# An attention and feed-forward kernel: the last whole group's sums and stores are listed ahead of the last products, and the steps behind unit 18 stand in a new order

## The chip, the cores and the metric

The kernel runs on one core of one Trainium2 chip. The metric is the device time of one execution in microseconds (us). Before the change it is 647.43 us, the median of three runs (647.06 to 649.99).

The engines are named as in the profile: PE is TensorE's matmul, PEld its weight load, DVE is VectorE, ACT is ScalarE, POOL is GpSimd, and SP is SyncE, whose queue issues most DMAs. Each engine works through its own list of instructions in order, and waits at an instruction until what it needs from the others is there.

## The reference

The first half is an attention over 32 memory slots for each of 8 batches and 8 heads (576 rows, 64 columns); the second is a feed-forward layer with a leaky ReLU on all 4608 rows:

```python
def _attn_ref(q, k, v, phi):
    a = np.exp(phi - np.max(phi, axis=2, keepdims=True))
    a = a / (np.sum(a, axis=2, keepdims=True) + 1e-09)
    k_m = np.einsum('bhsm,bhsd->bhmd', a, k)
    v_m = np.einsum('bhsm,bhsd->bhmd', a, v)
    scores = 1.0 / np.sqrt(q.shape[-1]) * np.matmul(q, k_m.transpose(0, 1, 3, 2))
    attn = softmax(scores)            # with 1e-09 in the denominator
    return np.matmul(attn, v_m)

x = attn_out.transpose(0, 2, 1, 3).reshape(4608, 512)
h = x @ w_in                          # w_in 512 x 2048
out = np.maximum(0.01 * h, h) @ w_out # w_out 2048 x 512
```

All arrays are float32.

## The kernel before

The program is one long list of named **steps**, written out in two tables of text, `OPENING` and `LATER`. At the end the kernel calls the steps in the order of the tables (`run(OPENING.split())`, `run(LATER.split())`) under a manual schedule: a step's instructions are put at the end of the lists of the engines that it uses. So the tables alone set the order of work on each engine. Two steps that use different engines don't delay each other by their order in the table; only the order within an engine, and the waits for data and buffers, count.

A step's name is a kind, a number and a part:

- `a2.C10`, `a6.E1` and so on are the attention of one batch. `phi`, `kv0` to `kv3`, `q0`, `q1` are its loads on SP. `A1` (line 595) and `A2` (610, 614) take the maxima of phi on DVE, `B...` the exponentials, `C10` (701) the products with k and v on PE, `D...` small transposes and scales (`D4`: 352 to 817; `D5`, `D6`: 823 and 828, the two halves of the operand vT), `E1`, `E3` (864) the scores on PE, `E20` to `E23` (909) their flips on DVE, and `S01` to `S08` (931 and on) the softmax.
- `W20` and the like fold w_in with the memory values of a batch (2) for a quarter of the hidden columns (0): `p` products on PE (1023), `h` high parts on ACT (1056), `l` low parts on DVE (1062). With it the up product runs on the attention weights.
- `i...` and `o...` prepare w_in and w_out: loads, rounding, splits into float16 high and low parts (419, 424, 444 to 450).
- Units 0 to 23 are the up and down products of the first two batches, in three groups of 384 rows: `P` up products on PE (1136), `V` leaky ReLU on ACT (1143), `C` and `L` high and low parts on DVE (1153, 1157), `O` down products on PE (1218). `Z` stores a group.
- Units 0 to 55 in small letters are the same for the other six batches, in 14 groups (G = 3 to 16) of 256 rows with 4 units each: `p` up products on PE (1263), `v` leaky ReLU on ACT (1279), `s` sums of its blocks on DVE (1300), `c` high parts on ACT (1304), `l` low parts on DVE (1308), `d` down products on PE (1331). A whole group takes seven block products instead of eight, so the results are sums of the seven: `x15.p` (ACT, 1341) and `x15.0` to `x15.3` (DVE, 1344, 1346, 1349, 1351) for group 15. `z15.0`, `z15.1` scale its two tiles of 128 rows (ACT, 1355) and store them: four DMAs of 64 KB each on SP (1185).
- Group 16 has 128 rows only (units 52 to 55). Its down products (line 1368) make two halves of 256 columns. `end0` scales the first half on ACT (1202), `end1` the second on DVE (1204); each half goes out in four DMAs of 32 KB, two from SP's queue and two from ACT's.

Up and down products in float16 run three times: high by high, high by low, low by high. So a `d` step of groups 3 to 15 is 6 matmuls of 128x256. The up products of groups 3 to 16 write two halves of one PSUM bank in turn, so `p52.2` must wait until `v52.0` has read what `p52.0` wrote. The operands of the down products lie in three buffers (`k % 3`), so unit 54's are written over unit 51's. The three PSUM banks of the down products are handed from one group to the next when the sums have read them.

Of the kernel before, what the change touches and what calls it, by code (L numbers as in the profile page):

```python
# [71 lines left out]
W01.l0 C9 o2.k0 a1.S12 o3.n3 P11.0 L9 V10.1 O8.1 a2.A3 o2.s1 o2.l0 o2.s2 P11.1 W01.h1 o2.k2 C10  # L72
# [14 lines left out]
a2.S05 i3.k2 a3.B10 i3.k0 a2.S06 O20.1 V22.0 a3.B20 W20.l0 W22.p W22.h0 W22.l0 a3.B3 O21.0 a3.C10
i3.l1 i3.l0 a2.S07 a3.C2 C22 a3.C30 a2.S08 p0.0 p0.1 O21.1 v0.0 p0.2 v0.2 L22 o1.n3 a3.C3k O22.0
a3.C31 v0.1 a4.phi i3.l2 a3.q0 V23.1 p0.3 C23 W23.p a3.C4 W23.h1 p1.0 v1.0 O22.1 v0.3 c0.0 p1.1 p1.2
W22.h1 L23 a4.A1 W23.h0 W23.l1 v1.2 s0 W23.l0 v1.1 a3.q1 c0.1 O23.0 p1.3 l0.0 W22.l1 a3.D2 v1.3  # L90
a3.D4 a3.D11 a3.D5 O23.1 p2.0 a3.D10 d0.0 l0.1 a3.Q1 p2.1 a3.Q0 Z2.0 d0.5 Z2.2 c1.0 a3.D6 v2.1 d0.3
v2.0 d0.4 l1.0 a3.D3 Z2.1 p2.2 a3.E1 a3.E22 a3.E3 s1 d0.1 a4.A2 v2.2 a3.E21 p2.3 p3.0 a3.E20 d1.0
# [5 lines left out]
a4.B3 p6.1 W31.h0 v6.1 x3.1 d4.1 a4.C10 a3.S07 p6.2 p6.3 a4.q1 s5 v6.2 d4.2 x3.2 v6.3 d3.6 l5.0
a4.C2 x3.3 d4.5 c5.1 p7.0 p7.1 a4.C30 a4.C31 d4.6 l5.1 v7.0 a4.q0 d5.0 p7.2 c6.0 d5.1 a3.S08 s6 v7.1
d5.5 d4.3 l6.0 v7.2 a4.C3k p7.3 p8.0 c6.1 d6.0 a4.D10 d4.4 a5.phi W31.l0 v7.3 d5.3 c7.0 l6.1 s7 p8.1  # L100
v8.1 d5.6 d6.5 d5.2 v8.0 a4.Q1 z3.1 l7.0 p8.2 z3.0 d6.1 a4.Q0 d5.4 a4.C4 a4.D3 d6.2 p8.3 a5.A1 v8.3
v8.2 c8.0 a4.E1 a4.E20 d7.0 c7.1 a4.E21 a4.E22 a5.A2 p9.0 v9.0 a5.A4 d6.3 a4.E3 l7.1 W32.p p9.1
W32.h0 s8 W32.h1 p9.2 v9.1 a4.E23 c8.1 d6.4 W32.l1 d7.1 a5.kv3 p9.3 a5.kv0 W32.l0 l8.0 v9.2 d6.6
# [6 lines left out]
d11.1 z4.0 s12 p13.1 d11.5 p13.2 v13.2 d11.0 d11.6 a5.B3 v13.1 W40.l0 W41.l1 c12.1 d10.3 p13.3 l12.1  # L110
v13.3 c12.0 a5.C10 d11.2 s13 l12.0 p14.0 p14.1 c13.0 v14.1 x5.p a5.q1 W41.l0 a4.S06 a5.C2 v14.0
d10.4 x5.0 c13.1 l13.0 d11.3 d11.4 d12.0 d12.1 p14.2 x5.1 x5.2 p14.3 a5.C30 d12.3 d12.2 x5.3 a4.S07
v14.2 v14.3 p15.0 p15.1 c14.0 v15.0 d12.4 v15.1 a5.C31 a5.C3k d12.5 a5.C4 p15.2 l14.0 a6.phi a5.D2
p15.3 a5.q0 d13.0 v15.2 v15.3 a5.Q1 l13.1 d12.6 s14 c15.0 a4.S08 z5.1 p16.0 d14.0 p16.1 v16.1 d13.1
# [18 lines left out]
p27.0 d23.6 d23.4 l25.0 v27.0 x8.0 a7.phi x8.1 v26.3 p27.1 x8.2 x8.3 c25.1 v27.1 a6.C4 d25.0 d24.5
p27.2 c26.0 p27.3 d24.3 d24.4 l25.1 a6.q1 v27.2 p28.0 s26 a6.C3k d24.6 d24.1 v27.3 a6.D10 l26.0
v28.0 c27.0 d24.2 c26.1 d25.1 d25.2 d25.3 d26.1 a6.Q0 p28.1 a6.Q1 a6.D3 p28.2 a6.E1 l26.1 v28.1
d25.4 a6.E20 d25.5 s27 p28.3 a6.D2 d26.3 z8.1 d25.6 d26.5 d26.6 v28.2 l27.0 p29.0 a6.D4 d26.4 c27.1
l27.1 a6.D11 a6.E21 v28.3 d26.2 v29.0 p29.1 z8.0 a6.D5 a7.A1 p29.2 c28.0 d26.0 v29.1 d27.0 d27.3
a6.D6 l28.0 a6.E22 d27.1 os5 s28 p29.3 W60.p a7.A2 a6.E3 v29.3 x9.p a6.E23 d27.2 x9.0 x9.1 a7.kv1
# [1387 lines left out]
```

## Time and profile before

| | us |
|---|---|
| median of three runs | 647.43 |
| the profiled execution's own time | 646.6 |
| its span (first to last instruction on the core) | 644.5 |
| PE busy | 626.9 (97%) |
| DVE busy | 526.7 (82%) |
| ACT busy | 383.7 (60%) |
| POOL busy | 33.8 (5%) |

The granted clock of TensorE was 0.997 of full speed over the span. The profile's groups give a line, engine, operation, tiles and count, then busy time and the mean of one, then the idle time of the engine ahead of them. A timeline row gives start, length, engine, line, operation and count; what stands in brackets is the engine's idle time ahead of it and who ended it. Ends of matmuls are modelled. `SPq` and `ACTq` are the issues of DMAs in these engines' queues.

### The profile page before, as it was taken

Reading aid. Unit: us, or ns where it says so; the run is one execution under the profiler, and the core shown is the slowest. Engines: PE = TensorE matmul, PEld = TensorE weight load, DVE = VectorE, ACT = ScalarE, POOL = GpSimd, SP = SyncE. Lnnn points to the kernel's source line nnn. Section 1 sums busy time; section 2 is a strip of 40 time slices with the busy share of each in tenths; the row PEclk is TensorE's granted clock in tenths of the full one; section 3 lists DMA queues with packets and bytes.
Section 4 is the critical chain, followed back from the end, with each engine's and each line's share of the span. In section 5 each row is a group of like instructions: output and inputs, shape, how many; then the busy total and the mean of one; then the engine's idle time right before and its main releaser. Section 6 shows DMA issues by size and latency. Waiting matters only on the chain.

```text
span 644.5 us, 17207 instructions
## 1 busy us (share of the span) xinstructions
PE 626.9 (97%) x7324; PEld 478.4 (74%) x7324; DVE 526.7 (82%) x870; ACT 383.7 (60%) x670; POOL 33.8 (5%) x38
## 2 busy tenths in 40 slices
PE   6799999999999999999999999999999999999996
...
GB/s 261 404 390 301 242 46 46 116 75 38 160 46 90 73 155 38 109 157 19 100 118 18 42 13 97 74 56 138 53 18 35 84 26 3 17 18 34 17 19 49
DMA packets 85500, 61.16 MB, mean 95 GB/s; under 512 B 62000, under 2 KB 68656, under 8 KB 85424
## 3 DMA queue, kind: packets, MB, share of 16 engines
...
q8 instruction: 57, 0.93, 0.6%
...
## 4 chain that ended last, share of the span: by engine, by line
PE 81%; DVE 10%; DMA 6%; ACT 2%; issue 1%; SPq 0%; DVEq 0%; ACTq 0%
PE po L1331 30%; PE ph L1263 21%; PE po L1218 11%; PE ph L1331 5%; PE ph L1136 4%; DMA arena<-in_moe_w_in_dram 4%; PE pa L1023 3%; PE pa L701 2%; PE po L1368 2%; PE pa L864 1%; DMA arena<-in_v_dram 1%; DVE arena L1300 1%; DVE arena L1157 1%; DVE arena L444 1%; DVE wo L424 1%
## 5 line engine op out<-in xcount | busy, mean ns | idle before, releaser
L1331 PEld LDWEIGHTS <-arena 128*128 128x128 f16 x2184 | 210.6, 98 | 29.2 <-issue 5.1
L1279 ACT ACTIVATE wi<-ph,g_sc 128x256 f32<-128x256 f32 (+1 forms) x224 | 96.1, 465 | 163.0 <-PE ph L1263 157.6
L1263 PE MATMUL ph<-a,w_mem 128*128 128x256 f16 (+3 forms) x1440 | 142.3, 246 | 0.5 <-ACT wi L1279 0.5
L1263 PEld LDWEIGHTS <-w_mem 128*128 128x128 f16 x1440 | 114.0, 98 | 15.4 <-issue 5.2
L1331 PE MATMUL po<-wo,arena 128*128 128x256 f16 x936 | 121.0, 273 | 0.4 <-DVE obs L1349 0.3
L1331 PE MATMUL po<-arena 128*128 128x256 f16 x936 | 120.0, 273 | 0.0
L1218 PE MATMUL po<-wo,arena 128*128 128x512 f16 (+1 forms) x396 | 107.6, 419 | 0.3 <-DVE arena L1157 0.3
L1308 DVE TENSOR_TENSOR arena<-arena 128x1024 f16<-128x1024 f32 x52 | 65.1, 1251 | 9.1 <-ACT arena L1304 9.1
L1308 DVE TENSOR_TENSOR arena<-wi,arena 128x768 f16<-128x768 f32 (+1 forms) x60 | 52.2, 878 | 22.4 <-ACT arena L1304 22.3
L1304 ACT CAST arena<-arena 128x1024 f16<-128x1024 f32 x52 | 54.3, 1045 | 9.0 <-DVE arena L1300 9.0
L1218 PEld LDWEIGHTS <-arena 128*128 128x128 f16 x324 | 31.1, 98 | 36.6 <-issue 2.5
L1300 DVE TENSOR_TENSOR arena<-wi 128x256 f32<-128x256 f32 x104 | 43.5, 459 | 5.0 <-ACT wi L1279 3.2
L1304 ACT CAST arena<-wi 128x768 f16<-128x768 f32 (+1 forms) x60 | 46.0, 774 | 2.2 <-PE po L1331 1.6
L1136 PE MATMUL ph<-a,w_mem 128*128 128x192 f16 (+2 forms) x288 | 46.9, 307 | 0.2 <-DVE w_mem L1062 0.2
L1300 DVE TENSOR_TENSOR arena<-wi,arena 128x256 f32<-128x256 f32 x104 | 43.8, 421 | 1.8
L988 POOL TENSOR_TENSOR a<-t,a 128x1024 f16<-128x1024 f32 (+2 forms) x16 | 23.8, 1506 | 407.8 <-ACT a L983 407.8
L1331 PE MATMUL ph<-wo,arena 128*128 128x256 f16 x312 | 42.1, 273 | 0.0
L1143 ACT ACTIVATE arena<-ph,g_sc 128x384 f32<-128x384 f32 x36 | 20.3, 577 | 20.3 <-PE ph L1136 18.9
L1136 PEld LDWEIGHTS <-w_mem 128*128 128x128 f16 x264 | 23.3, 98 | 10.8 <-issue 1.2
L1062 DVE SCALAR_TENSOR_TENSOR w_mem<-pa,w_mem 128x512 f16<-128x512 f32 x40 | 26.8, 683 | 4.8 <-ACT w_mem L1056 4.8
L1023 PE MATMUL pa<-wi,vT 64*32 64x512 f16 (+1 forms) x704 | 29.0, 420 | 1.0 <-ACT vT L808 1.0
L1056 ACT ACTIVATE w_mem<-pa 128x512 f16<-128x512 f32 x40 | 23.2, 597 | 5.9 <-PE pa L1023 5.9
...
## 6 DMA issues: line engine op xcount, KB each, us to landing
...
```

The source lines that it names most:

```text
L988: nc.gpsimd.tensor_tensor(piece(lo, tb), piece(t2, tb), piece(hi, tb), ALU.subtract)
L1023: nc.tensor.matmul(pf[g][cols, :], lhs, rhs, start=(n == 0), stop=(n == len(passes) - 1), tile_position=(g * D, hh * M),)
L1056: nc.scalar.activation(tiles(halves(w16(b, j), g)[:, 0]), w(g), AF.Copy, scale=ws)
L1062: nc.vector.scalar_tensor_tensor(tiles(t[:, 1]), w(g), ws, tiles(t[:, 0]), ALU.mult, ALU.subtract)
L1136: nc.tensor.matmul(ph[:, t0:t0 + n * SB], lhs, rhs, start=(m == 0), stop=(m == len(seq) - 1))
L1218: nc.tensor.matmul(pos["32" if full(G, u) else G][t], lhs, rhs, start=(f == 2 * u0 and m == 0), stop=(f == 2 * u1 - 1 and m == len(seq) - 1),)
L1263: nc.tensor.matmul(ph[:, t0:t0 + n], lhs, rhs, start=(m == 0), stop=(m == len(seq) - 1))
L1279: nc.scalar.activation(dst, ph, AF.Prelu, scale=g_sc2[:, j:j + 1], alpha=SLOPE)
L1300: nc.vector.tensor_tensor(gt[:, x], y, z, op)
L1304: nc.scalar.copy(dst[:, 0], src)
L1308: nc.vector.tensor_tensor(dst[:, 1], src, dst[:, 0], ALU.subtract)
L1331: nc.tensor.matmul(acc, g[:, x, s, u], rhs, start=(h == 0 and j == 0 and u == 0 and m == 0), stop=(j == NQ - 1 and u == 1 and m == 2), ski ...
```

## The change

Only the two tables of text are changed; every function stays as it is, and every step is called once, as before. `OPENING` has three moves in its middle: `i3.ld1` and `i2.h2` ahead of `u1.O1`, `o2.h2` and `a1.kv1` against their neighbours, `u3.V1` behind `a1.E1`. `LATER` has two moves ahead of unit 18 (`a2.A3`, `o0.k0`) and a new order from there to its last row. The steps `x15.3`, `z15.0` and `z15.1` stand behind `l55.1`, between `d54.2` and `d54.3`, before the change; they stand behind `p55.2` and from there to `d53.2` after it.

```diff
 OPENING = """
...
-o2.t0 i1.b f02.1 o2.h2 u2.P1 o2.y1 u3.V0 f02.2 u2.O0 a1.A1 a1.A2 u4.P0 a1.kv1 i3.h1 a1.A3 a1.B0
+o2.t0 i1.b f02.1 u2.P1 a1.kv1 o2.y1 u3.V0 f02.2 u2.O0 o2.h2 a1.A1 a1.A2 u4.P0 i3.h1 a1.A3 a1.B0
...
-a1.C31 u4.V1 u3.V1 a1.D3 i3.y0 u5.P0 a1.E1 a2.phi i3.h0 i3.t0 a1.C4 i3.h2 a1.E22 u3.O1 i3.y2 o3.ld2
+a1.C31 u4.V1 a1.D3 i3.y0 u5.P0 a1.E1 a2.phi u3.V1 i3.h0 i3.t0 a1.C4 i3.h2 a1.E22 u3.O1 i3.y2 o3.ld2
...
 LATER = """
...
-o0.n3 o0.n2 os1 i1.k2 P18.0 a2.E23 i1.l0 a2.E20 V18.0 C19 Z1.2 C18 L19 P21.0 P21.1 Z1.1 L18 Z1.0
-i1.k1 V21.1 i2.k0 a2.D11 O16.0 O16.1 O17.0 a2.E21 a2.S01 o0.m0 i0.l2 i1.l2 i1.l1 V21.0 P23.0 a2.D2
-i2.k1 a2.D4 a2.D5 O17.1 a3.kv2 P20.0 a3.kv0 C21 V20.0 L21 O18.0 V23.0 a2.D6 P20.1 V20.1 a3.A1 a3.A2
...
+o0.n3 o0.n2 os1 i1.k2 a3.kv2 a3.A1 a2.E21 P18.0 V18.0 C19 Z1.0 C18 a2.E20 Z1.1 Z1.2 P21.1 i1.l0
+P21.0 i1.k1 a3.kv0 O16.0 O16.1 L19 a2.E23 V21.0 V21.1 a2.D2 O17.0 i0.l2 O17.1 P23.0 i2.k0 a2.D11
+a2.D4 a2.S01 a3.A2 L18 i1.l2 i1.l1 a3.kv1 a2.D5 P20.0 a2.D6 O18.0 a3.A4 C21 W20.p V20.0 i2.k1 P20.1
...
-v51.1 p51.2 p51.3 z14.1 v51.3 l50.0 v51.2 l49.1 d49.5 s50 d49.1 c50.1 d48.4 c51.0 p52.0 p52.1 l51.0
-v52.0 d49.2 v52.1 d49.3 d49.4 c52.0 z14.0 p52.2 p52.3 l50.1 s51 d50.1 v52.2 d50.0 v52.3 p53.0 p53.1
-d50.3 c51.1 v53.0 d50.4 d50.2 v53.1 d49.6 p53.2 d51.1 l51.1 l52.0 v53.2 c52.1 d51.3 d50.5 d51.2
-p53.3 p54.0 d51.0 v53.3 d50.6 p54.1 x15.p d51.4 c53.0 x15.0 d51.5 v54.1 v54.0 x15.1 p54.2 l53.0
-p54.3 l52.1 v54.3 v54.2 d51.6 x15.2 c54.1 c53.1 d52.0 p55.0 d52.1 d52.2 d52.3 c54.0 d53.0 v55.0
-l54.0 p55.1 l53.1 p55.2 l54.1 d53.1 v55.2 v55.1 c55.0 l55.0 d53.2 d53.3 d54.0 d54.1 p55.3 v55.3
-d54.2 c55.1 l55.1 x15.3 z15.0 z15.1 d54.3 d55.0 d55.1 end0 d55.2 d55.3 end1
+l50.0 d48.4 d49.3 p51.2 p51.3 v51.3 d48.1 d48.2 d48.6 d49.4 v51.2 p52.0 p52.1 s50 c50.1 c51.0 l50.1
+s51 z14.0 d49.1 v52.0 v52.1 c51.1 d49.0 p52.2 p52.3 v52.2 v52.3 d49.2 d50.1 d50.2 p53.0 d50.3 d50.4
+l51.1 z14.1 c52.0 d50.0 p53.1 v53.1 v53.0 d51.3 l51.0 d51.0 d49.5 x15.p p53.2 p53.3 d51.1 l52.0
+v53.2 v53.3 d51.2 p54.0 p54.1 x15.0 d51.4 v54.1 c53.0 x15.1 v54.0 x15.2 d49.6 d50.5 p54.2 p54.3
+c52.1 l53.0 d52.0 d52.1 c54.0 l52.1 v54.2 v54.3 p55.0 p55.1 v55.0 d52.2 d52.3 v55.1 d50.6 d51.5
+d51.6 c53.1 l53.1 c54.1 p55.2 x15.3 p55.3 v55.2 d53.0 d53.1 l54.1 l54.0 v55.3 c55.0 l55.0 z15.0
+d53.2 z15.1 c55.1 l55.1 d53.3 d54.0 d54.1 d54.2 d54.3 d55.0 d55.1 end0 d55.2 d55.3 end1
 """
```

More of the change, by code (lines that the diff above doesn't have):

```diff
@@ L71 @@
 o2.m0 P10.0 V9.1 L8 W01.h0 P10.1 i0.k0 Z0.1 W11.p Z0.0 o3.s3 o3.m3 o2.n0 Z0.2 o2.k1 V10.0 O8.0
[L72 removed]
+W01.l0 C9 o2.k0 a1.S12 o3.n3 a2.A3 P11.0 L9 V10.1 O8.1 o2.s1 o2.l0 o2.s2 P11.1 W01.h1 o2.k2 C10
 W01.l1 a1.S13 O9.0 a2.B10 V11.0 o2.m1 o2.m2 o2.n1 W11.h1 V11.1 L10 O9.1 o2.s3 a2.kv0 W11.h0 W11.l1
@@ L77 @@
 P14.0 C13 o1.s1 o1.n0 L13 V14.0 O11.1 o1.m1 o1.s2 P14.1 V14.1 a1.S18 C14 O12.0 o1.n1 o1.s3 L14 a2.B3
-P15.0 o1.l2 o1.m2 O12.1 V15.0 o0.k0 P16.1 V16.1 P15.1 o1.n2 P16.0 a2.C2 a3.phi o0.l0 a2.C30 V15.1
+P15.0 o1.l2 o1.m2 O12.1 V15.0 P16.1 o0.k0 V16.1 P15.1 o1.n2 P16.0 a2.C2 a3.phi o0.l0 a2.C30 V15.1
 C15 o0.s3 P17.1 V16.0 C16 o0.s0 L16 o0.k1 a2.C3k o0.l1 o0.s1 O13.0 o0.k2 L15 a2.Q1 o0.l2 O13.1 O14.0
@@ L87 @@
[L87 to L92, printed above, removed]
@@ L98 @@
[L98 to L103, printed above, removed]
@@ L110 @@
[L110 to L114, printed above, removed]
@@ L133 @@
[L133 to L138, printed above, removed]
@@ new lines @@
+P21.0 i1.k1 a3.kv0 O16.0 O16.1 L19 a2.E23 V21.0 V21.1 a2.D2 O17.0 i0.l2 O17.1 P23.0 i2.k0 a2.D11
+a2.D4 a2.S01 a3.A2 L18 i1.l2 i1.l1 a3.kv1 a2.D5 P20.0 a2.D6 O18.0 a3.A4 C21 W20.p V20.0 i2.k1 P20.1
+a2.S02 W20.h1 O18.1 W20.l1 L21 V20.1 i2.l1 i2.k2 a2.S03 o1.m3 i2.l0 W20.h0 a3.A3 W21.p C20 i2.l2 L20
+P22.0 O19.0 O19.1 i3.k2 W20.l0 W21.h1 O20.0 V22.0 a2.S04 W21.l1 W21.h0 a3.B10 o0.m0 P22.1 W22.p
+a2.S05 i3.k0 W21.l0 a2.S06 i3.k1 V23.0 O20.1 O21.0 i3.l1 V22.1 P23.1 W22.h0 W22.l0 a3.B20 a3.B3
+a3.C10 a3.C2 a2.S07 a2.S08 p0.0 V23.1 o1.n3 p0.1 C23 O21.1 W22.h1 i3.l0 v0.0 v0.1 p0.2 C22 a3.C30
@@ new lines @@
+a3.C3k L22 i3.l2 p0.3 v0.3 v0.2 o0.n0 O22.0 a3.C31 a3.C4 c0.0 l0.0 p1.0 p1.1 a4.phi v1.0 O22.1 a3.q0
+a3.D2 v1.1 L23 a3.D10 s0 p1.2 a3.D4 W22.l1 a3.D11 p1.3 a3.D5 a3.D6 v1.3 O23.0 a3.q1 v1.2 p2.0 a3.Q0
+a4.A1 W23.p v2.0 c0.1 a3.Q1 O23.1 l0.1 p2.1 p2.2 d0.0 W23.h1 W23.l1 W23.h0 W23.l0 Z2.2 d0.5 v2.1 s1
+Z2.0 a3.D3 a4.A2 p2.3 d0.1 d0.6 v2.3 a3.E1 a3.E22 v2.2 Z2.1 c1.1 c1.0 a3.E3 p3.0 p3.1 d0.2 a3.E23
+a3.E20 d0.3 l1.0 W30.p v3.1 v3.0 d1.1 p3.2 l1.1 p3.3 a3.E21 s2 c2.0 d1.0 v3.3 a3.S01 l2.0 W30.h1
@@ new lines @@
+W30.l1 v3.2 c3.0 c2.1 l3.0 a4.A4 l2.1 d0.4 d1.3 a4.A3 p4.0 p4.1 d2.0 v4.1 W31.p v4.0 s3 d1.2 p4.2
+d1.5 a4.kv0 v4.2 d1.6 d2.5 W31.h1 c3.1 a4.kv1 d3.0 a3.S02 W31.h0 W30.h0 p4.3 l3.1 p5.0 v4.3 v5.0
+d1.4 d2.3 d2.1 a4.kv3 a4.B10 p5.1 x3.p p5.2 d2.6 a3.S03 os2 c4.0 s4 v5.2 c4.1 W31.l1 v5.1 d2.2 d3.1
+d3.2 d2.4 l4.0 p5.3 W31.l0 l4.1 d3.5 p6.0 a4.kv2 a4.B20 d3.3 a4.C10 a3.S04 a3.S05 v5.3 c5.0 x3.0
+v6.0 p6.1 d3.4 v6.1 d3.6 p6.2 p6.3 l5.0 a4.B3 a4.C2 a3.S06 W30.l0 x3.1 s5 x3.2 d4.0 d4.1 d4.2 v6.3
+a3.S07 v6.2 x3.3 d5.1 c5.1 p7.0 p7.1 c6.0 l5.1 v7.1 a4.q0 a4.C30 a5.phi a3.S08 d4.5 d4.3 d4.6 d5.0
@@ new lines @@
+v7.0 p7.2 p7.3 a4.C3k d4.4 a4.D10 d5.5 l6.0 d5.6 v7.3 v7.2 p8.0 p8.1 a4.C31 s6 c7.0 a4.q1 v8.0 d5.3
+a4.Q0 d5.2 c6.1 p8.2 a5.A1 d6.0 v8.1 a4.D3 l7.0 d5.4 p8.3 v8.2 v8.3 c8.0 a4.Q1 l6.1 s7 d6.1 a4.E1
+d6.3 z3.0 z3.1 a4.E22 a4.E20 p9.0 p9.1 d6.5 a4.E3 a4.E21 a4.C4 c7.1 W32.p v9.0 W32.h1 l7.1 d7.0
+a4.E23 p9.2 W32.h0 a5.A2 W32.l0 d6.2 a5.kv3 v9.1 W32.l1 v9.2 d6.4 a4.D2 p9.3 v9.3 a4.D4 W33.p W33.h0
+d7.1 s8 d6.6 a4.D11 p10.0 l8.0 d7.2 x4.p d7.3 c8.1 a4.D5 c9.0 d7.5 W33.l0 p10.1 d7.4 d8.0 v10.0
+v10.1 l8.1 p10.2 a4.D6 x4.0 p10.3 l9.0 W33.h1 W33.l1 os3 W40.p a5.A4 v10.2 d8.5 p11.0 W40.h1 s9
@@ new lines @@
+p14.1 p14.2 a5.q1 x5.p x5.0 x5.1 v14.1 d12.0 d12.3 v14.2 p14.3 x5.2 l13.0 d12.1 d12.2 a5.C30 p15.0
+d12.4 s13 c13.1 a5.C3k d13.1 x5.3 v15.0 d12.5 d13.0 v14.3 p15.1 p15.2 d12.6 l13.1 d13.5 s14 W41.l0
+a5.Q0 a5.C31 a6.kv0 d13.6 a5.C4 c14.0 l14.0 a4.S08 v15.2 v15.1 p15.3 v15.3 c15.0 a5.Q1 d13.2 d13.3
+p16.0 z5.1 a5.D2 a5.D4 v16.0 a5.D10 a5.D3 c14.1 d14.0 p16.1 l14.1 a5.E1 v16.1 p16.2 p16.3 d14.5
+v16.3 l15.0 s15 d14.1 a6.phi d13.4 v16.2 p17.0 a5.E21 c15.1 a5.E20 d14.3 p17.1 z5.0 d14.2 l15.1
+v17.0 d14.6 a5.E22 v17.1 p17.2 s16 d14.4 a5.E3 W42.p c16.0 p17.3 d15.1 d15.2 W42.h0 W42.h1 a6.A1
@@ new lines @@
+W52.h1 v24.3 W51.l1 W52.l1 c23.1 W52.l0 a6.B20 p25.0 l23.1 s24 p25.1 v25.1 v25.0 z7.0 c24.0 d22.2
+W53.p p25.2 p25.3 c24.1 W53.h0 a6.B3 v25.2 d22.4 l24.1 x8.p d22.6 W53.l0 d23.3 l24.0 p26.0 v25.3
+c25.0 d23.1 d23.2 a6.C10 v26.0 a6.q1 s25 W53.h1 W53.l1 p26.1 a6.C2 a6.C30 c25.1 a6.C31 a6.C4 l25.0
+p26.2 d23.4 v26.2 d23.5 x8.0 x8.1 v26.1 p26.3 v26.3 d23.6 c26.0 d24.0 p27.0 p27.1 x8.2 l26.0 d24.5
+a7.phi v27.1 a6.D2 x8.3 v27.0 d24.1 a6.q0 p27.2 p27.3 v27.2 d24.6 l25.1 s26 d24.2 d25.1 v27.3 c27.0
+d25.2 p28.0 p28.1 z8.0 a7.A1 l27.0 d25.5 a6.C3k v28.0 d24.3 p28.2 c26.1 v28.2 d24.4 a6.D10 a6.Q0
@@ new lines @@
+v31.3 l30.1 W61.h1 p32.0 p32.1 d29.1 a6.S01 a6.S02 v32.0 W61.l1 W60.l1 v32.1 a7.A4 d29.2 d30.1 p32.2
+p32.3 a6.S03 s31 c31.1 l31.1 v32.3 d29.5 a6.S04 v32.2 c31.0 l31.0 s32 W62.p d29.6 os6 a6.S05 z9.1
+d30.5 p33.0 d30.6 d31.5 c32.0 p33.1 d30.3 d30.4 z9.0 v33.0 W61.l0 v33.1 p33.2 p33.3 d30.0 d30.2
+d31.1 d31.2 v33.3 a6.S06 W62.h1 W62.l1 v33.2 a7.A3 c33.0 l32.0 W62.h0 W62.l0 d31.3 c32.1 a7.B10
+d31.0 x10.p x10.0 p34.0 l32.1 d31.6 l33.0 a6.S07 p34.1 d32.0 d31.4 v34.0 p34.2 d32.1 d32.2 d33.1
+v34.2 v34.1 a7.B20 s33 c33.1 p34.3 p35.0 v34.3 W63.p W63.h1 x10.1 x10.2 d32.5 p35.1 a7.kv1 v35.1
```

116 lines of the change are left out of this document (50 added, 66 removed).

## The prediction

> **What bounds the kernel now.** I read the page's busy shares first, then the stages (busy time of each engine in a stretch), then TensorE's waits behind unit 17, then the timeline of the last 8 us.
>
> ```profile
> PE 626.9 (97%) x7324; PEld 478.4 (74%) x7324; DVE 526.7 (82%) x870; ACT 383.7 (60%) x670; POOL 33.8 (5%) x38
> ...
> PE   6799999999999999999999999999999999999996
> ```
>
> TensorE (PE) is busy 97% of the span. Only the first two slices and the last one show room.
>
> ```profile
> 160.00:240.00 80.00, 80.00 (x850) 50.49 (x849) 74.09 (x125) 47.03 (x82) 3.29 (x3) 1.00 0.41 106
> 240.00:260.00 20.00, 19.71 (x304) 17.32 (x303) 19.27 (x29) 11.33 (x21) 2.77 (x4) 1.00 0.27 43
> 380.00:400.00 20.00, 19.36 (x260) 15.82 (x257) 16.08 (x25) 14.99 (x26) 0.00 (x0) 1.00 0.29 88
> 600.00:620.00 20.00, 20.00 (x207) 18.17 (x205) 10.08 (x16) 11.13 (x22) 0.00 (x0) 1.00 0.11 28
> 620.00:640.00 20.00, 18.12 (x193) 16.31 (x190) 5.42 (x12) 7.15 (x19) 0.00 (x0) 1.00 0.09 22
> 640.00:644.50 4.50, 0.00 (x0) 0.00 (x0) 0.00 (x0) 0.00 (x0) 0.00 (x0) 0.59 0.34 83
> ```
>
> The columns behind the length are PE, weight loads, DVE, ACT and POOL, then the granted clock. From 160 us to TensorE's end it stands still in two stretches alone: 20 − 19.71 = 0.29 and 20 − 19.36 = 0.64, together 0.93 us. In 160 to 240 us DVE works 74.1 of 80 us, so it is nearly a second bound there; at the end it has much room. The order of the steps ahead of unit 18 is almost untouched, so the opening's loss stays. What an order can win is then 0.93 us of stalls, and the tail:
>
> ```profile
> 633.69 0.50 PE L1263 MATMUL ph<-a,w_mem 128*128 128x128 f16 x6
> 634.02 4.09 PE L1368 MATMUL po<-wo,arena 128*128 128x256 f16 x36
> 634.22 0.37 ACT L1279 ACTIVATE wi<-ph,g_sc 128x128 f32<-128x128 f32 x1 [2.45 <-PE ph L1263]
> 634.62 0.40 ACT L1304 CAST arena<-wi 128x256 f16<-128x256 f32 x1
> 635.06 0.43 DVE L1308 TENSOR_TENSOR arena<-wi,arena 128x256 f16<-128x256 f32 x1 [2.82 <-ACT arena L1304]
> 635.40 0.68 DVE L1351 TENSOR_TENSOR obs<-po,obs 128x512 f32<-128x512 f32 x1
> 636.12 1.33 ACT L1355 ACTIVATE obs<-obs,osc 128x512 f32<-128x512 f32 x2 [1.09 <-DVE obs L1351]
> 636.87 5.46 SPq L1185 DMA_DIRECT2D out_dram<-obs  x12
> 637.36 0.45 ACT L1202 ACTIVATE obs<-po,osc 128x256 f32<-128x256 f32 x1
> 637.84 1.79 ACTq L1185 DMA_DIRECT2D out_dram<-obs  x4
> 638.15 0.48 DVE L1204 TENSOR_SCALAR obs<-po,osc 128x256 f32<-128x256 f32 x1 [2.07 <-PE po L1368]
> ```
>
> TensorE ends at 634.02 + 4.09 = 638.11 us, and the last result is in SBUF at 638.63. The span is 644.5. What ends last is SP's queue: 12 output DMAs in a row from 636.87 to 642.33, 5.46/12 = 0.455 us each. The first eight store group 15 (z15.0 and z15.1); they become ready only when the last sum L1351 (x15.3) and the scalings L1355 are done, and the half tile's own four stores queue behind them. The last one starts at 641.9:
>
> ```profile
> L1185 SPq DMA_DIRECT2D out_dram<-obs x1: 419/419/419, 641.9 to 641.9; - x1
> ...
> DMA to landing us min/median/max: 1.6/1.6/1.6
> ```
>
> It lands at 643.5, and 1.0 us later the span ends.
>
> **The tail, part by part.** Nothing is added or taken out; every engine issues the same instructions. On DVE, the last rows before (wi_89 and arena hold the hidden values and their parts, obs the results):
>
> ```order
> L1308 TENSOR_TENSOR arena<-wi_89,arena 128x256 x2
> L1349 TENSOR_TENSOR obs<-obs,po 128x2x256
> L1308 TENSOR_TENSOR arena<-wi_89,arena 128x256 x5
> L1351 TENSOR_TENSOR obs<-po,obs 128x512
> L1204 TENSOR_SCALAR obs<-po,osc 128x256
> ```
>
> and the last rows on DVE now:
>
> ```order
> L1349 TENSOR_TENSOR obs<-obs,po 128x2x256
> L1308 TENSOR_TENSOR arena<-wi_89,arena 128x256 x3
> L1351 TENSOR_TENSOR obs<-po,obs 128x512
> L1308 TENSOR_TENSOR arena<-wi_89,arena 128x256 x4
> L1204 TENSOR_SCALAR obs<-po,osc 128x256
> ```
>
> L1351 no longer stands behind the last low parts L1308 (l55.0, l55.1). On ScalarE, the last rows ahead of its DMAs before:
>
> ```order
> L1304 CAST arena<-wi_89 128x256
> L1279 ACTIVATE wi_89<-ph,g_sc_101 128x128
> L1304 CAST arena<-wi_89 128x256
> L1355 ACTIVATE obs<-obs,osc 128x512 x2
> L1202 ACTIVATE obs<-po,osc 128x256
> ```
>
> and the same place on ScalarE now:
>
> ```order
> L1279 ACTIVATE wi_89<-ph,g_sc_101 128x128 x2
> L1304 CAST arena<-wi_89 128x256
> L1355 ACTIVATE obs<-obs,osc 128x512 x2
> L1304 CAST arena<-wi_89 128x256
> L1202 ACTIVATE obs<-po,osc 128x256
> ```
>
> The two L1355 moved ahead of the last cast (c55.1), and the table lists both up products p55.2 and p55.3 ahead of the last twelve down steps.
>
> A down step is 6 matmuls, 4.09 less the 0.2 us of the last one's drain over 6 steps, 0.65 us; an up step is 634.02 − 633.69 = 0.33. TensorE now ends its list with 12 down steps (d53 to d55) behind p55.2, p55.3 and d51.6. Counted back from an unchanged end, d51.6 is issued by 638.11 − 12 × 0.655 − 0.66 = 629.6, and its consumer starts 0.2 later (p55.3: issued by 634.02, L1279 at 634.22). So L1351 runs 629.8 to 630.5. The move adds a wait on ScalarE: d50.6 and d51.6 now stand behind the first products of unit 52, and c53.1 and c54.1 overwrite the operands that these two read (each unit's operands use the buffer of the unit three before). c54.1 is therefore held until 629.8 and ends at 630.2. Queued behind it are v55.2, v55.3 (0.37 each; p55.3 is issued by 630.25), c55.0 (0.40) and L1355 twice (1.33): 630.95, 631.35, 632.7. Who waits for them are d55.0 at 635.3, which is far off, and SP. SP's eight stores run from 632.1 for 8 × 0.455 = 3.6 us, to 635.7, and SP is free 3 us before the last half needs it. Behind L1355 stand c55.1 and then l55.1: done by 632.7 + 0.40 + 0.43 = 633.5, while d55.1, which reads it, is issued three steps before the end, at 636.0. So that costs nothing; if this cover of 2.5 us were gone, TensorE would stand still for what is missing.
>
> Then only the half tile is left. Its first half, L1202, can follow d55.1 at 636.8 instead of 637.36, and its four stores go out while d55.2 and d55.3 run. L1204 still ends at 638.63. SP and ScalarE's queue have two stores each behind it; the second starts at 638.67 + 0.455 = 639.1. They land 1.5 to 1.9 us after their start (those on ACT's queue 1.8, which I take), so 640.9, and with the 1.0 us at the end the span is 641.9 instead of 644.53: **2.6 us less**. The bounds are 2.4 (landing after 2.1, the slowest of the last stores) and 2.8 (1.6).
>
> The Trainium skill (Perfetto Trace Analysis, section "DMA Instruction — HWDGE") says that an issue locks the descriptor generator, which sequencers share. By that rule the last four stores would go out one by one, the last at 640.05, and the gain would be 1.7. The trace disagrees: ACT's four stores took 1.79 us, 0.45 each, while SP issued at 0.455.
>
> **The new order from unit 18 on.** TensorE's work in this stretch is the same, so an order can only make or mend stalls. The largest shift that I found is on DVE at 165 us. Before and now, one piece of the difference:
>
> ```order
>  L817 TENSOR_SCALAR sv<-sv 128x1
> -L1153 CAST arena<-arena 128x768
> -L1157 TENSOR_TENSOR arena<-arena 128x768
> +L931 TENSOR_REDUCE tm<-t_1776 128x36
> +L610 STREAM_TRANSPOSE r1k<-r1k 128x128
> +L614 TENSOR_REDUCE mx_1905<-r1k 128x4
> +L1157 TENSOR_TENSOR arena<-arena 128x768
> +L424 SCALAR_TENSOR_TENSOR wi_86<-wi_87,sw,wi_86 128x512
> +L424 SCALAR_TENSOR_TENSOR wi_86<-wi_87,sw,wi_86 128x768
>  L828 SCALAR_TENSOR_TENSOR vT<-pa,sv,vT 128x128
> ```
>
> The added L1157 is L18, the low part that TensorE's O18.0 reads. It moves behind batch 3's phi maxima (L595, L610, L614) and other work:
>
> ```profile
> 167.53 1.82 DVE L1157 TENSOR_TENSOR arena<-arena 128x768 f16<-128x768 f32 x2
> 169.27 0.71 DVE L909 STREAM_TRANSPOSE t<-pa 128x512 f32<-128x512 f32 x1
> 170.02 1.35 DVE L931 TENSOR_REDUCE tm<-t 128x36 f32<-128x1152 f32 x1
> 171.28 2.46 DVE L424 SCALAR_TENSOR_TENSOR wi<-wi,sw,wi 128x512 f16<-128x512 f32 x3
> 173.66 0.28 DVE L352 TENSOR_REDUCE pv<-pa 128x1 f32<-128x128 f32 x1
> ...
> 174.36 0.15 DVE L817 TENSOR_SCALAR sv<-sv 128x1 f32<-128x1 f32 x1
> ...
> 176.62 0.34 DVE L828 SCALAR_TENSOR_TENSOR vT<-pa,sv,vT 128x128 f16<-128x128 f32 x1
> 176.88 2.14 DVE L595 TENSOR_REDUCE r1k<-arena 128x128 f32<-128x1152 f32 x1
> 179.05 0.31 DVE L610 STREAM_TRANSPOSE r1k<-r1k 128x128 f32<-128x128 f32 x1
> ```
>
> ```profile
> 176.00 2.11 PE L1218 MATMUL po<-wo,arena 128*128 128x512 f16 x9
> 177.94 2.11 PE L1136 MATMUL ph<-a,w_mem 128*128 128x384 f16 x12
> ...
> 182.80 0.84 PE L1023 MATMUL pa<-wi,vT 64*32 64x512 f16 x24
> ```
>
> L18 ended at 169.35. Ahead of it come L595 2.17 (start to start), L909 0.71, L931 1.26, one L424 0.8, the four steps L352 to L817 0.85, and L610 with L614 about 0.7: 6.5 us, so about 175.8. O18.0 (the 9 matmuls at 176.00) has the same work ahead of it as before. A cover of 6.6 us shrinks to 0.2. The fold W20.p moves up from 182.80 to directly behind O18.0, 177.94; it needs L828, now two L424 behind L18: 175.8 + 1.6 + 0.34 = 177.75, again 0.2 to spare. So this costs nothing if DVE never idles, and some tenths if it does once. The other places that I followed have covers of the old kind: a bank of up products is refilled no sooner than three steps (about 1.6 to 2 us) after it was written, in both orders.
>
> Per place I bound a stall by nothing and by the longest of the old ones, 0.4 us:
>
> ```profile
> PE ph L1263 <- ACT wi L1279: 0.5, 2, 0.4
> PE po L1331 <- DVE obs L1349: 0.3, 1, 0.3
> ```
>
> The four old stalls summed to 0.93 and come at other places now. The net runs from −0.93 (none left) to +1.9 (three times as many). I take **+0.2**, near the old level, since DVE's covers at 176 us became thinner.
>
> **The sum.** 644.53 − 2.6 + 0.2 = 642.1 of span. The profiled execution took 646.6 around its 644.5; the median of the runs shown is 647.43, 0.8 above it. The same difference, −2.4, from the median gives **645.0 us**, 0.4% faster. The likeliest case alone spans 644.3 to 646.4.
>
> **The rivals.**
>
> *More than the tail (chance 0.18).* The search also mends the stalls: 647.43 − 2.6 − 0.93 = 643.9. For it: 0.93 us is there to be had. Against: DVE's thin cover at 176 us. The Trainium skill (Perfetto Trace Analysis, section "Identifying the Most-Contended Engine") calls matmul busy time a poor measure and points to the share of weight loads, 74% here. By that rule there is more room than 0.93 us; the trace puts it inside the steps, since a down step keeps its 0.65 us wherever it stands.
>
> *DVE becomes the bound in units 18 to 23 (0.10).* Between 160 and 240 us DVE idles 80 − 74.09 = 5.9 us, in waits. If the new order makes it wait as much but ahead of L18, L828 and the low parts that follow, TensorE waits with it, because the covers are 0.2 us. A third of it is 2.0; it decides from 2.6 on, where it eats the tail's gain. At 60%, 3.5 us, the time is 647.43 − 2.6 + 3.5 = 648.3, slower than before. Against it: DVE's waits were for TensorE's scores (L909), and the flips now stand later.
>
> *The stores still come last (0.06).* If L1355 waited until 635.0 or later, SP's 3.6 us would again push the half tile's stores. That takes 2.3 us of delay against the 632.7 above, for instance when v55.3 or c55.0 waits for a buffer. If all of the gain went, 647.6.
>
> **Chances and range.** Forecast 0.66, rivals 0.18, 0.10 and 0.06. A run of this kernel can tell about 0.5%, 3.2 us, from no change: below 644.2 is faster, above 650.7 slower. The first rival lies almost wholly below 644.2, and a few hundredths of the forecast do: faster 0.20. Slower needs over 5.9 us of new stalls, more than the second rival's price: 0.05. The rest, 0.75, is no change. The range 643.5 to 647.6 leaves out the second rival and the far end of the first.
>
> **What would show it.** In the changed profile: SP's last stores begin at about 638.7 and not in one row of twelve; L1351 runs about 8 us ahead of TensorE's end; the span ends about 3.8 us behind TensorE, not 6.4. Behind 160 us, PE's windows lose about 1 us in all. I am wrong if TensorE's end moves by over 1 us from 638.1 (then the stalls decide, and the window with the loss names the place), or if the tail stays near 6 us.

## The result and the profile after

| | before | after |
|---|---|---|
| median of five runs each, side by side, us | 647.62 | 644.1 (643.41 to 645.38) |
| ratio, 95% interval | | 0.9941 (0.9919 to 0.9963) |
| the profiled execution's own time, us | 646.6 | 644.1 |
| its span, us | 644.5 | 642.1 |

The change makes the kernel 0.59% faster, 3.5 us. The forecast was 645.0; the time lies inside the range 643.5 to 647.6 and nearest to the rival "more than the tail" (643.9). It is 0.2 us below the stretch of the likeliest case alone (644.3 to 646.4).

The page of the changed kernel, busy times and PE's row of slices:

```profile
PE 629.4 (98%) x7324; PEld 479.7 (75%) x7324; DVE 523.2 (81%) x870; ACT 383.7 (60%) x670; POOL 33.8 (5%) x38
...
PE   7799999999999999999999999999999999999997
```

PE is still the bound, and the only slices with room are still the first two and the last. The stages of the changed kernel (columns as before the change: PE, weight loads, DVE, ACT, POOL, granted clock):

```profile
160.00:240.00 80.00, 80.00 (x848) 50.36 (x846) 72.81 (x122) 46.45 (x84) 2.56 (x3) 1.00 0.39 106
240.00:260.00 20.00, 20.00 (x309) 17.78 (x307) 19.30 (x31) 10.80 (x20) 3.80 (x4) 1.00 0.37 72
...
380.00:400.00 20.00, 20.00 (x225) 17.61 (x223) 15.57 (x24) 11.61 (x22) 3.10 (x3) 1.00 0.06 15
```

The 0.29 us missing at 240 to 260 us and the 0.64 us at 380 to 400 us are gone, and no such gap appears in 160 to 240 us. Up to PE's end, the windows behind 160 us lose only 0.07 us now, at 480 to 500 us. The timeline of the last 13 us of the changed kernel:

```profile
629.85 0.40 ACT L1304 CAST arena<-wi 128x256 f16<-128x256 f32 x1 [0.96 <-PE po L1331]
629.90 0.69 DVE L1351 TENSOR_TENSOR obs<-po,obs 128x512 f32<-128x512 f32 x1 [0.56 <-PE po L1331]
631.38 1.34 ACT L1355 ACTIVATE obs<-obs,osc 128x512 f32<-128x512 f32 x2
632.14 7.59 SPq L1185 DMA_DIRECT2D out_dram<-obs  x12
...
637.12 0.47 ACT L1202 ACTIVATE obs<-po,osc 128x256 f32<-128x256 f32 x1 [4.11 <-PE po L1368]
637.63 2.17 ACTq L1185 DMA_DIRECT2D out_dram<-obs  x4
638.43 0.48 DVE L1204 TENSOR_SCALAR obs<-po,osc 128x256 f32<-128x256 f32 x1 [4.96 <-PE po L1368]
```

and the stores alone, from 636 us on (duration in ns, then first and last start):

```profile
L1185 SPq DMA_DIRECT2D out_dram<-obs x4: 315/368/422, 637.6 to 639.3; - x4
L1185 ACTq DMA_DIRECT2D out_dram<-obs x4: 374/408/432, 637.6 to 639.4; - x4
...
DMA to landing us min/median/max: 1.5/1.6/1.7
```

The last sum L1351 runs 8.5 us ahead of L1204, not 2.75 us. SP sends group 15 long before the end, and only the half tile's stores are left behind 637 us; the last one starts at 639.4 instead of 641.9.

**Taking the difference apart.** Each execution can be cut at two rows: the 48 score matmuls of L864 right ahead of unit 18's first product, and the copy L1204, which follows PE's last matmul by 0.04 us. L864 in the kernel before, then in the changed one:

```profile
161.85 1.23 PE L864 MATMUL pa<-arena,x_k 64*32 64x64 f32 x48
```

```profile
162.71 1.23 PE L864 MATMUL pa<-arena,x_k 64*32 64x64 f32 x48
```

| us, profiled execution | opening: to L864 | middle: L864 to L1204 | tail: L1204 to the span's end |
|---|---|---|---|
| before | 161.85 | 638.15 − 161.85 = 476.30 | 644.5 − 638.15 = 6.35 |
| after | 162.71 | 638.43 − 162.71 = 475.72 | 642.1 − 638.43 = 3.67 |
| difference | +0.86 | −0.58 | −2.68 |

The sum is −2.40, the two spans' difference. The start of unit 18 scatters by more than this +0.86 in either order, as the experiments show, so I leave it out. Without it the change is worth −2.68 − 0.58 = −3.3 us, close to the medians' 3.5.

### The profile page after: what moved, and what is told of

It is laid out like the page before. It is cut to its first block, busy times and chain, and to the rows that moved or that the text cites. A ratio compares the mean times of both kernels' runs of the same rounds, so it can differ in the third digit from the quotient of the medians.

```text
span 642.1 us, 17210 instructions
## 1 busy us (share of the span) xinstructions
PE 629.4 (98%) x7324; PEld 479.7 (75%) x7324; DVE 523.2 (81%) x870; ACT 383.7 (60%) x670; POOL 33.8 (5%) x38
## 4 chain that ended last, share of the span: by engine, by line
PE 89%; DVE 5%; DMA 3%; ACT 1%; issue 0%; SPq 0%; ACTq 0%
PE po L1331 32%; PE ph L1263 22%; PE po L1218 14%; PE ph L1136 6%; PE ph L1331 5%; PE pa L1023 4%; PE pa L701 2%; DMA arena<-in_moe_w_in_dram 2%; PE po L1368 2%; PE pa L864 1%; DVE arena L1157 1%; DVE arena L444 1%; DMA wo<-in_k_dram 1%; DVE wo L424 1%; DVE arena L450 1%; DVE arena L1153 0%
## 5 line engine op out<-in xcount | busy, mean ns | idle before, releaser
L1308 DVE TENSOR_TENSOR arena<-arena 128x1024 f16<-128x1024 f32 x52 | 63.8, 1227 | 21.8 <-ACT arena L1304 21.6
L1308 DVE TENSOR_TENSOR arena<-wi,arena 128x768 f16<-128x768 f32 (+1 forms) x60 | 55.5, 931 | 18.3 <-ACT arena L1304 18.2
L1300 DVE TENSOR_TENSOR arena<-wi,arena 128x256 f32<-128x256 f32 x104 | 45.7, 439 | 1.8
L988 POOL TENSOR_TENSOR a<-t,a 128x1024 f16<-128x1024 f32 (+2 forms) x16 | 23.8, 1505 | 405.5 <-ACT a L983 405.5
L1300 DVE TENSOR_TENSOR arena<-wi 128x256 f32<-128x256 f32 x104 | 39.6, 422 | 1.7 <-ACT wi L1279 0.6
```

Of the source, the lines that this page charges most:

```text
L988: nc.gpsimd.tensor_tensor(piece(lo, tb), piece(t2, tb), piece(hi, tb), ALU.subtract)
L1300: nc.vector.tensor_tensor(gt[:, x], y, z, op)
L1308: nc.vector.tensor_tensor(dst[:, 1], src, dst[:, 0], ALU.subtract)
```

## The experiments

My theory, one: the gain has two independent parts, the tail (about 2.6 us) and the stalls behind unit 18 (0.6 to 0.9). Rivals: the tail alone with a lucky opening; a new opening that helps; the order alone. The four kernels of the first group ran side by side; the kernel before had a median of 647.24 us there.

**The tail alone.** The kernel before, with only the three steps of group 15 moved:

```diff
-p54.3 l52.1 v54.3 v54.2 d51.6 x15.2 c54.1 c53.1 d52.0 p55.0 d52.1 d52.2 d52.3 c54.0 d53.0 v55.0
-l54.0 p55.1 ...
-d54.2 c55.1 l55.1 x15.3 z15.0 z15.1 d54.3 d55.0 ...
+p54.3 l52.1 v54.3 v54.2 d51.6 x15.2 x15.3 c54.1 c53.1 d52.0 p55.0 d52.1 d52.2 d52.3 c54.0 d53.0 v55.0
+z15.0 z15.1 l54.0 p55.1 ...
+d54.2 c55.1 l55.1 d54.3 d55.0 ...
```

> The kernel before with three steps moved and nothing else: x15.3 directly behind x15.2, z15.0 and z15.1 behind v55.0. Theory one (the tail and the stalls add up; SP's queue of twelve stores is all that the tail lost): the span ends 3.8 us behind TensorE's end instead of 6.4, TensorE's end stays, the stalls stay at 0.9 us, and the time is 2.6 us below before, near 645.0. Theory two (the new order as a whole makes the gain, and the last stores would land late anyway): the tail stays above 5 us and the time is within 1 us of before.

Measured: 644.96 us, ratio 0.9963 (0.9947 to 0.9979), 2.3 us faster. Its timeline and its PE waits behind 150 us:

```profile
627.04 0.69 DVE L1351 TENSOR_TENSOR obs<-po,obs 128x512 f32<-128x512 f32 x1 [0.29 <-PE po L1331]
...
638.86 0.48 DVE L1204 TENSOR_SCALAR obs<-po,osc 128x256 f32<-128x256 f32 x1 [2.67 <-PE po L1368]
```

```profile
PE ph L1263 <- ACT wi L1279: 0.5, 2, 0.4
PE po L1331 <- DVE obs L1349: 0.3, 1, 0.3
```

The tail is 642.5 − 638.86 = 3.64 us, that of the changed kernel. The waits are those of the kernel before, and so is the middle: 638.86 − 162.54 = 476.32 against 476.30. Three moved steps give the whole of the tail's part, and nothing of the other.

**The order alone.** The changed kernel with the end of its table as it was: the last up product, its cast and low part late again, and the sum and the stores behind them.

```diff
-d51.6 c53.1 l53.1 c54.1 p55.2 x15.3 p55.3 v55.2 d53.0 d53.1 l54.1 l54.0 v55.3 c55.0 l55.0 z15.0
-d53.2 z15.1 c55.1 l55.1 d53.3 d54.0 d54.1 d54.2 d54.3 ...
+d51.6 c53.1 l53.1 c54.1 p55.2 v55.2 d53.0 d53.1 l54.1 l54.0 c55.0 l55.0 d53.2 d53.3
+d54.0 d54.1 p55.3 v55.3 d54.2 c55.1 l55.1 x15.3 z15.0 z15.1 d54.3 ...
```

> The changed kernel with the end of its table as before: p55.3, v55.3, c55.1 and l55.1 late, then x15.3, z15.0, z15.1. Theory one: the tail is 6.4 us again and the stalls behind 160 us stay near 0.1 us, so the time is 2.6 us above the changed kernel and 0.9 below before, near 646.7. Theory two: it keeps most of the 3.5 us, near 644.5.

Measured: 647.38 us, ratio 0.9994 (0.9975 to 1.0012). The median can't tell 0.9 us from nothing, and the interval holds both. The profile tells more. Its timeline:

```profile
637.33 0.68 DVE L1351 TENSOR_TENSOR obs<-po,obs 128x512 f32<-128x512 f32 x1
...
640.08 0.48 DVE L1204 TENSOR_SCALAR obs<-po,osc 128x256 f32<-128x256 f32 x1 [2.07 <-PE po L1368]
```

The tail is back (647.0 − 640.08 = 6.92 us), while the middle is short: L864 stands at 164.73, so 640.08 − 164.73 = 475.35 us, 0.95 less than before.

**The opening.** The changed kernel with the opening and the rows ahead of unit 18 as before (the diff is the reverse of the change's first rows).

> The changed kernel with OPENING and the rows of LATER ahead of unit 18 as before. In the profiled executions unit 18 came 0.86 us later in the changed kernel than in the one before, for TensorE began its first work and the next steps later. If that is the scatter between executions: same time as the changed kernel within 0.4 us, and a start of unit 18 that scatters as well. If the opening's moves cost it: 0.8 us below the changed kernel, near 643.3.

Measured: 643.94 us, ratio 0.994 (0.9917 to 0.9964), the changed kernel's own. The moves ahead of unit 18 are worth nothing that can be seen. The interval is 3 us wide, though, so a cost or a gain of some tenths is not excluded. L864 stands at 161.04 to 163.98 us in the five profiles with the old opening, and at 161.73 to 166.58 in the seven with the new one.

**Two entries by hand.** The tail's edit on the kernel before, and two steps moved out of the way at the old stalls:

```diff
-... p6.3 a4.q1 s5 v6.2 d4.2 x3.2 v6.3 ...
+... p6.3 a4.q1 x3.2 s5 v6.2 d4.2 v6.3 ...
-c20.1 l20.1 d18.6 a5.S07 d19.3 ... c21.0 v22.3 d19.5 ...
+c20.1 l20.1 d18.6 d19.3 ... c21.0 v22.3 a5.S07 d19.5 ...
```

> tail_only, and two steps more moved, where TensorE stood still in the kernel before: x3.2 ahead of s5 (d4.5 waited for it at 254 us), and a5.S07 behind v22.3 (it stood ahead of v22.1 and v22.2 on ScalarE, and p23.0 and p23.2 waited for those at 382 to 386 us). Theory one: both stretches lose nothing now, or under 0.2 us, and the time is that of the changed kernel within 0.5 us, near 644.2. Theory two (stalls move on and come back elsewhere, only the whole search removes them): the windows at 240 to 260 and 380 to 400 us get better, others get worse by as much, and the time stays near 645.0.

Measured: 643.62 us, ratio 0.9936 (0.991 to 0.9961). Its trace has no PE wait behind 150 us, and the middle is 635.94 − 161.04 = 474.90 us, 1.4 less than with the tail's edit alone, where the windows show only 0.93 us of idle time in all. Aligned step by step on PE (the starts of the same instructions in both traces), it gains 0.45 us at 254 us, where the trace shows a wait of 0.29, and 0.27, 0.42 and 0.27 at three places between 380 and 387 us, where the windows show 0.64. That is the whole 1.4, and at the old stalls alone.

**Which part of the tail's edit carries it?** The changed kernel also has p55.2 and p55.3 earlier. Here it is with the sum and the stores listed behind the last low part again:

```diff
-d51.6 c53.1 l53.1 c54.1 p55.2 x15.3 p55.3 ... l55.0 z15.0
-d53.2 z15.1 c55.1 l55.1 d53.3 ...
+d51.6 c53.1 l53.1 c54.1 p55.2 p55.3 ... l55.0 d53.2 c55.1 l55.1
+x15.3 z15.0 z15.1 d53.3 ...
```

> The changed kernel with the last sum and the stores of group 15 (x15.3, z15.0, z15.1) listed behind the last low part l55.1 again, as before the change, while the last up products keep their early place. Theory one (SP's row of twelve stores ends the span, so the gain is only what it starts earlier): l55.1 ends at 633.5, so L1351 ends at 634.2, SP starts at about 635.0 and its twelve stores of 0.455 us go out in one row again, the last at 640.0 instead of 639.3; the span ends 4.5 to 4.8 us behind TensorE instead of 3.8. So most of the tail's gain comes from the early up products, and about 0.8 us from listing the sum and the stores ahead. Rival a (the listing is what counts): the tail returns to 6.4 us. Rival b (the stores have slack to spare either way): it stays at 3.8 us.

Measured, one run: 644.39 us beside 645.45 of the kernel before, and a tail of 642.2 − 638.49 = 3.71 us. Rival b held, and my 0.8 us was wrong. The timeline shows why:

```profile
632.26 0.69 DVE L1351 TENSOR_TENSOR obs<-po,obs 128x512 f32<-128x512 f32 x1
632.98 1.33 ACT L1355 ACTIVATE obs<-obs,osc 128x512 f32<-128x512 f32 x2 [1.13 <-DVE obs L1351]
633.73 6.05 SPq L1185 DMA_DIRECT2D out_dram<-obs  x12
...
638.49 0.48 DVE L1204 TENSOR_SCALAR obs<-po,osc 128x256 f32<-128x256 f32 x1 [5.55 <-PE po L1368]
```

L1351 runs at 632.26 and not at 633.5, since the last casts no longer queue behind L1355. SP starts its eight stores at 633.73 and is done with them at 633.73 + 8 × 0.455 = 637.4, 0.3 us before the first half is ready (L1202 ends at 637.65). Between the two kernels the sum moved by 2.4 us and the end did not. So either half of the edit is enough: with late up products the sum must be listed ahead (the tail alone, 3.64 us), with early ones it need not be (3.71), and with neither the tail is 6.4 to 6.9 us.

**One queue for the half tile.** The changed kernel with this line:

```diff
-rows, eng = out[b * S:(b + 1) * S, es], nc.scalar if last is not None and y % 2 else nc.sync
+rows, eng = out[b * S:(b + 1) * S, es], nc.sync
```

> The changed kernel with all eight stores of the last half tile on SP's queue instead of every second one on ScalarE's. Theory of two queues that issue side by side at 0.45 us a store: SP's last eight stores begin at 637.6 and go out in one row, the last one starting at about 640.8 instead of 639.3, so the span ends 5.0 to 5.4 us behind TensorE instead of 3.8. By the rule that the Trainium skill (Perfetto Trace Analysis, section "DMA Instruction - HWDGE") states, an issue locks a descriptor generator that the sequencers share; by that rule the eight stores would already go out one by one, and nothing changes: 3.8 us.

Measured, one run: 646.43 us, with a tail of 644.4 − 639.40 = 5.00 us instead of 3.67. Its stores, and L1202 ahead of the last eight:

```profile
638.09 0.47 ACT L1202 ACTIVATE obs<-po,osc 128x256 f32<-128x256 f32 x1 [4.11 <-PE po L1368]
639.40 0.48 DVE L1204 TENSOR_SCALAR obs<-po,osc 128x256 f32<-128x256 f32 x1 [4.96 <-PE po L1368]
```

```profile
L1185 SPq DMA_DIRECT2D out_dram<-obs x16: 314/420/529, 633.1 to 641.7; - x16
```

The first half is ready at 638.56, and the eighth store behind it starts at 641.7: one row at 3.1/7 = 0.45 us. Two queues do send side by side here, and this is worth 1.3 us. The Trainium skill's rule of a lock shared by the sequencers (Perfetto Trace Analysis, section "DMA Instruction — HWDGE"), read as a lock for the whole of an issue, would leave the tail at 3.7 us; this run's 5.00 us disagrees. A lock that is held for less than half of the 0.45 us is not excluded.

**The thin cover at 176 us.** A cover is the time from where an operand is ready to where it is used. The changed kernel with L18 listed two folds later on DVE:

```diff
-a2.D4 a2.S01 a3.A2 L18 i1.l2 i1.l1 a3.kv1 ...
+a2.D4 a2.S01 a3.A2 i1.l2 i1.l1 L18 a3.kv1 ...
```

> The changed kernel with L18 (L1157, the low part that O18.0 reads) listed behind the next two folds on DVE (i1.l2 and i1.l1, L424). Theory of the thin cover: L1157 ended at 175.99 and O18.0 began at 176.86, a cover of 0.87 us; two L424 of 0.8 us each take 1.6 us of it, so TensorE waits 0.5 to 1.0 us at O18.0 for L1157, and the way from the first up product of unit 18 to TensorE's end, 474.5 us in the changed kernel, grows by as much. Rival (DVE idles ahead of L18, so the order there costs nothing): no wait at O18.0, 474.5 us again.

Where L18 stood in the changed kernel:

```profile
175.04 0.95 DVE L1157 TENSOR_TENSOR arena<-arena 128x768 f16<-128x768 f32 x1
...
176.86 2.11 PE L1218 MATMUL po<-wo,arena 128*128 128x512 f16 x9
```

and with L18 late:

```profile
175.62 0.95 DVE L1157 TENSOR_TENSOR arena<-arena 128x768 f16<-128x768 f32 x1
175.88 0.59 PE L1218 MATMUL po<-wo,arena 128*128 128x512 f16 x2
...
176.63 1.69 PE L1218 MATMUL po<-wo,arena 128*128 128x512 f16 x7 [0.16 <-DVE arena L1157]
```

The wait appears, but small: two of the nine matmuls run without L18, and the trace shows 0.16 us for the rest. Aligned step by step on PE, this execution falls back by 0.32 us there against the changed kernel's. Below my 0.5 to 1.0, but the mechanism is the expected one. Its middle, 637.49 − 161.73 = 475.76 us, is hardly longer than the 475.72 of the changed kernel's first profile, which lost as much elsewhere, as the next runs show.

**Both again, side by side.** The changed kernel and the one with two entries by hand, five rounds each.

> The changed kernel unaltered, timed beside the next one on one chip, since its five runs gave 644.1 us with an interval of 0.4%. If the sum of the two terms found so far is right (2.6 us of the tail, 0.8 us of stalls behind unit 18), it stands 3.4 us below the kernel before: ratio 0.9947, near 644.0 us where the kernel before takes 647.4. If the tail alone counts, 0.9960, near 644.8 us.

> The kernel before with the three steps of group 15 listed ahead of the last down steps and two table entries moved for the stalls at 253.8 and 382.5 us, timed beside the changed kernel. From its profile (unit 18's first product to the span's end in 477.4 us against 478.3 of the changed kernel and 481.5 of the kernel before) I expect 4.0 us below the kernel before, ratio 0.9938, and 0.3 to 0.9 us below the changed kernel, which may not show beside the scatter of the opening. Rival: the whole search found more than two moved entries can, and this kernel is slower than the changed one by 0.5 us or more.

Measured: the changed kernel 643.66 us, ratio 0.9931 (0.9914 to 0.9948); the hand-made one 0.9937 (0.9914 to 0.996). The interval of the changed kernel takes in 0.9947, the two terms together, and leaves out 0.9960, the tail alone. The two kernels can't be told apart, so whether the new order as a whole gives more than the two entries stays open at this size; both beat the kernel before. The second profile of the changed kernel shows a wait that its first had not shown:

```profile
330.86 1.38 DVE L839 STREAM_TRANSPOSE arena<-arena 128x1152 f32<-128x1152 f32 x1 [2.98 <-DMA arena<-in_q_dram]
331.35 0.30 PE L864 MATMUL pa<-arena,x_k 64*32 64x64 f32 x4
332.29 1.27 PE L864 MATMUL pa<-arena,x_k 64*32 64x64 f32 x36 [0.63 <-DVE arena L839]
```

In its first profile the same place reads

```profile
330.60 1.38 DVE L839 STREAM_TRANSPOSE arena<-arena 128x1152 f32<-128x1152 f32 x1 [2.30 <-DMA arena<-in_k_dram]
331.77 1.53 PE L864 MATMUL pa<-arena,x_k 64*32 64x64 f32 x40
```

and in the kernel before

```profile
327.89 1.38 DVE L839 STREAM_TRANSPOSE arena<-arena 128x1152 f32<-128x1152 f32 x1 [0.22 <-issue]
...
332.62 1.23 PE L864 MATMUL pa<-arena,x_k 64*32 64x64 f32 x48
```

Before, the transposed queries of batch 5 were ready at 329.27, 3.35 us ahead of their matmuls. In the new order they are ready at 331.98, behind the start of the matmuls at 331.77, and these take 1.53 us, where the order alone, with the queries ready 1 us ahead, took 1.18. The new order spent a cover of 3.35 us. Its rows show a loss of 0.35 and 0.63 us; aligned step by step with the run of the late stores, where these queries are ready 0.1 us ahead, PE falls back by 0.32 us there in the first profile and by 0.99 in the second.

**A mend for it that brought another wait.** The changed kernel with these matmuls three places later:

```diff
-... d14.0 p16.1 l14.1 a5.E1 v16.1 p16.2 p16.3 d14.5
+... d14.0 p16.1 l14.1 v16.1 p16.2 p16.3 d14.5 a5.E1
```

> The changed kernel with one scoring step of batch 5 (a5.E1, the matmuls of L864 near 332 us) listed three places later on TensorE, behind two up steps and a down step (0.33 + 0.33 + 0.65 = 1.3 us). Theory of the late query load: in the changed kernel L839 waits there for the load of batch 5's queries, ends at 331.98, and L864 begins at 331.77 and takes 1.53 us instead of 1.18 (0.63 us of wait shown in its second profile); with 1.3 us more cover L864 waits no more whatever the opening takes, and from the 48 matmuls of L864 ahead of unit 18 to the last copy L1204 it takes 475.1 to 475.4 us, not 475.7 or 476.4; the median is 0.3 to 0.8 us below the changed kernel's. Rival: the scatter of the changed order (475.1 to 476.4) has another place, and the segment comes out anywhere in it.

Measured: 645.86 us, ratio 0.9964 (0.9943 to 0.9984), and a middle of 642.64 − 166.58 = 476.06 us. This is no gain over the changed kernel's 0.9931 and 0.9941. That it is slower is not shown: the intervals overlap, and the two were not timed side by side. Its PE waits, in a window from 150 us on:

```profile
PE ph L1263 <- ACT wi L1279: 0.6, 1, 0.6
PE pa L715 <- DVE r1k L679: 0.2, 1, 0.2
```

The first ends at p16.2 (336.27 us): without the 1.2 us of scores between them, p16.2 starts only 0.06 us after ACT has read what p16.1 wrote (335.74 to 336.21), the other half of the same bank. The step had been the cover of another wait. This takes back 0.56 us of the middle by the row, and 0.68 when aligned with the run of the late stores. The second wait ends at 149.68 us, ahead of L864, and is no part of the middle. This opening was the slowest of all (L864 at 166.58). The queries were ready at 334.67 us, ahead of the old place of their matmuls behind p16.1 (335.71); so the run shows the new wait, but not what the old one would have cost in it.

## Why the prediction was right, and where it was not

- **The tail**: predicted −2.6 (−2.4 to −2.8), measured 6.35 − 3.67 = 2.68, and alone 6.35 − 3.64 = 2.71. Its steps hold one by one: L1351 predicted 629.8 to 630.5, measured 629.90 to 630.59; c54.1 held until 629.8, measured 629.85; L1355 done at 632.7, measured 632.72; SP's eight stores from 632.1, measured 632.14; the second half's second stores at 639.1, measured 639.3 and 639.4; span end without the stalls' term 641.9, measured 642.1. L1204 stood 0.28 us later than before (638.43), where the sum took it as unmoved.
- **The wait of the queue as the cause** held too, but the margin was read too narrowly. I argued from the listing of the sum; the early up products alone give the same, since the real condition is only that SP has sent eight stores before the first half is ready.
- **The net of the stalls, +0.2, is the term that failed, in its sign too.** I bounded it by −0.93 and +1.9 and chose near the old level, "since DVE's covers at 176 us became thinner". Measured: the middle became 0.58 us shorter in the profile that goes with the result. So what came is nearer to the rival "more than the tail", which had a chance of 0.18. Seven profiles with the new order from unit 18 on (the changed kernel twice, the order alone, the old opening, the late stores, the late L18, one queue) have middles from 475.12 to 476.39 us against 476.30 and 476.32 with the old one: six gain 0.5 to 1.2, one loses 0.1. The old stalls at 254 us and at 381 to 386 us are gone in each.
- **The cover at 176 us** was read rightly as thin, at 0.2 us, and wrongly as a danger. It is 176.86 − 175.99 = 0.87 us in the trace, and 1.6 us of delay put on it cost 0.32. The rival of a bound on DVE is not seen: PE is busy 80.00 of 80 us there.
- **The larger new stall was at a place that I had passed over**, batch 5's queries at 332 us, where a load decides and not a bank. "Covers of the old kind" was said of places that I followed on ACT and DVE; I had not followed SP's list of loads behind unit 18. A second one, at the down products of 478.6 and 481.4 us, costs the six other profiles 0.27 to 0.29 us more than the run of the late stores; PE waits there for DVE, which one slow step holds up, as the last section shows. The two account for the spread of the middles: from the 475.12 of the late stores, the changed kernel's first profile (475.72) is 0.32 + 0.29 us longer, and its second (476.39) 0.99 + 0.27.
- **0.93 us as all that is there** was too little: two moved entries regained 476.32 − 474.90 = 1.4 in one profile and 476.32 − 475.20 = 1.1 in another, which again gained 1.4 at the old stalls and lost 0.3 at another place. Idle time shown between modelled matmul ends understated here what a stall costs.
- **The stores as the last thing still** is not seen. The signs named for a right forecast all came (last stores not in one row of twelve, L1351 8 us ahead, the end 3.7 us behind PE), except that PE lost 0.07 us, and not about 1, in its windows behind 160 us.
- The span's forecast, 642.1, met the measured one exactly, by two misses that cancel, which is luck: −0.8 on the stalls, +0.86 from a later opening. The forecast of the median, 645.0, was 0.9 us too high, about the size of the miss on the stalls.
